# A new written order for the first two tiles of a windowed-attention and squared-ReLU kernel

## The chip, the cores and the metric

The kernel runs on one core of a Trainium2 chip. The metric is device time in microseconds (us) of one execution. The kernel before takes 847.6 us, the median of three executions (847.17 to 847.6).

## What is computed

The reference runs attention over a window of 64 positions and hands its output, seen as 4608 tokens of 512 values, to a feed-forward layer with a squared ReLU between two matrix products. All inputs are float32.

```python
scores = scale * np.matmul(q, k.transpose(0, 1, 3, 2))      # q, k, v: (8, 8, 576, 64)
mask = (rel >= 0) & (rel < window)                          # window = 64
attn = softmax(np.where(mask, scores, -1e9))
x = np.matmul(attn, v).transpose(0, 2, 1, 3).reshape(4608, 512)
h = x @ w_in                                                # (512, 2048)
r = np.maximum(h, 0.0)
out = (r * r) @ w_out                                       # (2048, 512)
```

## The kernel before

The 4608 tokens are cut into 12 tiles of 384. Attention is done in sections, three for each tile; a section is four pieces of 64 queries by two heads by two halves. The hidden size of 2048 is cut into 16 blocks f of 128. A wide product is made of three products of split operands: a high part and a rest.

Tiles 0 and 1 and the first two blocks of tile 2 are handled by a table of tokens, a string called `order` (line 488). It is walked once, from left to right, and every token issues its instructions at once to the queue of its engine; each engine then runs its own queue strictly in that order, and waits where data are missing. So the table fixes the order on TensorE, VectorE (DVE), ScalarE (ACT), GpSimd (POOL) and on SP, which issues all transfers. What follows the table is ordered by a planner with costs and due times (class Plan), which is not touched; its instructions follow the table's on every engine. Its first ones on TensorE are the first product of step 34, the scores of section 10 and the values of section 9.

A token is a letter, a number n and for some tokens the engine (d VectorE, a ScalarE, p GpSimd):

- Loads on SP: `L` and `N` q and k of 128 tokens of batch 0 and 1 (line 185), `w` the two halves of weight block n (lines 104, 105), `v` values (157), `q` raw q and k of later batches (147), `B` writes weight block n back to memory for later (519), `W` writes an output tile (457).
- Attention of the first tokens: `T`, `U` transposes on TensorE (196), `t`, `u` the copies out of their banks (202). `D` turns raw q and k of later batches on VectorE (167).
- Section n: `S` scores on TensorE (235), `o` copy of half of them (243), `s` the masked other half (252, 253), `z` row maximum (255), `y` its scaling, `e` and `f` four exponentials each on ScalarE (263), `k`, `R` the reciprocal of the sums (266, 269), `m` the weighting (272), `X` transposes (276), `x` their masked copy on VectorE (280), `V` product with the values (298), `H` the high part and `Q` the rest of the result (313, 315), which is the input of the feed-forward layer.
- Weight block n, which arrives as pairs of 32-bit words: `a` on ScalarE (118), `b` two instructions, `c`, `d` on VectorE (120, 121, 123, 125), `h` the high part on ScalarE (129), `l` the rest on VectorE (132). Two blocks at most are between `a` and `l`.
- Step n (a pair of tile and block): `M` the first product, 12 matmuls (404), into one bank that all steps share; `r` ReLU on ScalarE (413), `p` square (416 or 418), `g` high part on ScalarE (421), `G` rest on VectorE (423), `O` the second product, 9 matmuls (446). Steps 0 to 4 are tile 0 with blocks 0 to 4, steps 5 to 9 tile 1 with the same blocks, and steps 10 to 22 are tile 1 with blocks 5 to 15 and, in two of them, tile 0. Step 22 ends tile 1, step 31 tile 0; steps 32 and 33 are tile 2. `Z` copies the finished tile out (455).
- `K` n filler matmuls on constants, on TensorE (512), whose result nobody reads.

There are eight semaphores for the transfers in turn, so a transfer is issued only when the eighth one before it has landed.

Of the kernel before, what the change touches and what calls it, by code (L numbers as in the profile page):

```python
# [29 lines left out]
def window_attention_relu2_ffn(ctx: ExitStack, tc: tile.TileContext, q, k, v, w_in, w_out, out):  # L30
    nc = tc.nc
    pe, dve, act, pool, sp = nc.tensor, nc.vector, nc.scalar, nc.gpsimd, nc.sync
# [73 lines left out]


    def weight(op, f):
        if op == "a":
            wa[f] = a_t[:, f % 2].bitcast(I32)  # L110
        a = wa[f]
        if op in "acd":
            words = wraw[f].rearrange("p n (e w) -> p w (n e)", w=2)
            lower, upper = words[:, 0, :], words[:, 1, :]
        else:
            av = a.bitcast(F32).rearrange("p (n e) -> p n e", n=2)
        if op == "a":
            act.activation(a.bitcast(F32), upper.bitcast(F32), AF.Abs, scale=2.0 ** -80)
        elif op == "b":
            dve.tensor_scalar(a.bitcast(F32), a.bitcast(F32), 1.875 * 2.0 ** -64, 2.0 ** -95, ALU.min, ALU.max)  # L120
            dve.tensor_scalar(a, a, 4, 1, ALU.logical_shift_left, ALU.logical_shift_right)
        elif op == "c":
            dve.scalar_tensor_tensor(a, lower, 29, a, ALU.logical_shift_right, ALU.bitwise_or)  # L123
        elif op == "d":
            dve.scalar_tensor_tensor(a, upper, -0x80000000, a, ALU.bitwise_and, ALU.bitwise_or)  # L125
# [25 lines left out]
    def load_v(b, t, which=None):  # L151
        vt = vts[b, t] = vt_t[:, t]
        for n in range(min(2, NB - 2 * t)):
            s0 = (2 * t + n) * QB
            for m in range(2):
                if not which or (n, m) in which:
                    sp.dma_start(vt[m * QB:(m + 1) * QB, n],  # L157
                                 v[b, m * H // 2:(m + 1) * H // 2, s0:s0 + QB, :].rearrange("h s d -> s h d"))
# [251 lines left out]
    def evac(op, n, eng=None):  # L410
        if op == "r":
            rg[n] = r_t[:, n % 2]
            act.activation(by_half(rg[n]), ordered(hs.pop(n)), AF.Relu)  # L413
        elif op == "p":
            if eng == "a":
                act.activation(rg[n], rg[n], AF.Square)
            else:
                dve.tensor_tensor(rg[n], rg[n], rg[n], ALU.mult)
        elif op == "g":
            gs[n] = (ghi_t[:, n % 3], glo_t[:, n % 2])  # L420
            act.copy(gs[n][0], rg[n])  # L421
        else:
            dve.tensor_tensor(gs[n][1], rg.pop(n), gs[n][0].bitcast(F32), ALU.subtract)  # L423

# [63 lines left out]
    order = """
        L0 L1 w0 L2 T0 v0 T1 t0a t1d S0 w1 T2 o0a T3 K5 t2d v1 s0 t3d a0 z0 S1 L3 y0 b0 f0 N0 T4 K3 c0 o1a L4
        t4a s1 T5 K5 e0 w2 d0 t5a N1 k0 z1 h0 S2 R0 y1 v2 m0d e1 l0 X0 K6 o2a x0 a1 v3 s2 V0 f1 b1 H0a k1 T6 K4  # L490
        w3 z2 R1 y2 t6d m1p v4 f2 Q0 T7 X1 c1 t7a U0 e2 x1 S3 u0a k2 d1 V1 o3a T8 v5 H1a R2 s3 m2p t8a T9 a2 Q1
        X2 t9d z3 h1 U2 K2 w4 b2 y3 u2a U1 K4 f3 w5 x2 u1a w6 c2 U3 e3 S4 w7 l1 u3a V2 k3 o4a v6 R3 H2a s4 m3p
        Q2 S5 a3 z4 X3 o5a b3 M0 y4 f4 x3 e4 c3 V3 r0 k4 d2 p0a M1 v7 H3a g0 R4 Q3 m4p h2 s5 X4 r1 G0 p1a z5 O0
        g1 x4 y5 e5 G1 V4 d3 f5 O1 v8 l2 H4a k5 h3 R5 Q4 m5p M2 a4 l3 w8 w9 X5 r2 b4 a5 M3 w10 x5 p2a w11 g2 c4
        r3 V5 w12 p3a G2 g3 w13 d4 O2 w14 G3 h4 H5d O3 w15 l4 q0 Q5 a6 M4 b5 b6 r4 M5 p4a c5 g4 q1 c6 r5 M6 p5a
        G4 g5 d6 O4 r6 d5 h6 G5 p6a M7 h5 g6 l5 O5 r7 G6 a7 l6 p7a O6 b7 g7 a8 G7 M8 c7 b8 O7 r8 p8a d7 g8 M9 G8
        h7 c8 O8 r9 l7 p9a g9 d8 a9 M10 G9 h8 b9 O9 r10 l8 p10a g10 c9 a10 B0 M11 G10 b10 O10 r11 p11a d9 g11 B1
        M12 G11 h9 c10 O11 r12 l9 p12a g12 d10 a11 B2 M13 G12 h10 b11 O12 r13 l10 p13a g13 c11 a12 B3 M14 G13
        b12 O13 r14 p14a d11 g14 B4 M15 G14 h11 c12 O14 r15 l11 p15a g15 d12 a13 B5 M16 G15 h12 b13 O15 r16 l12
        p16a g16 c13 a14 B6 M17 G16 b14 O16 r17 p17a d13 g17 B7 M18 G17 h13 c14 O17 r18 l13 p18a g18 d14 a15 B8  # L500
        M19 G18 h14 b15 O18 r19 l14 p19a g19 c15 B9 M20 G19 D0 O19 r20 p20a d15 q2 g20 M21 G20 h15 D1 O20 r21
        l15 p21a g21 q3 G21 M22 O21 r22 p22d g22 G22 M23 D2 O22 r23 p23d q4 g23 M24 G23 Z22 W22 O23 r24 p24d g24
        G24 S6 M25 o6a D3 q5 s6 O24 r25 z6 p25a y6 g25 f6 G25 S7 O25 e6 o7d s7 v9 k6 z7 M26 R6 y7 m6p f7 D4 X6
        e7 q6 S8 x6 r26 k7 V6 R7 o8a p26d m7p M27 H6a s8 g26 Q6 z8 X7 r27 G26 y8 M28 p27a x7 e8 D5 O26 g27 f8
        G27 q7 V7 r28 k8 R8 p28a m8p S9 g28 H7d M29 G28 Q7 o9d v10 X8 r29 s9 M30 p29a x8 g29 z9 v11 V8 r30 D6 y9
        f9 M31 p30d H8a e9 Q8 O27 k9 R9 m9p G29 O28 g30 r31 p31d X9 G30 g31 O29 x9 D7 G31 M32 O30 r32 p32d g32
        M33 G32 O31 r33 Z31 W31 p33d g33 G33"""
# [588 lines left out]
```

## Time and profile before

| what | before |
|---|---|
| median of three executions | 847.6 us |
| the profiled execution | 847.38 us |
| its span, first to last instruction | 845.1 us |
| busy: TensorE, VectorE, ScalarE, GpSimd | 829.0, 590.5, 407.3, 184.9 us |
| first matmul of the table | 4.26 us |
| first product of step 0 (`M0`) starts | 39.85 us |
| last second product of the table (`O31`) starts, ends | 185.74, 187.68 us |
| mean granted TensorE clock | 0.998 |

The span is the time from the first to the last instruction; the 2.28 us between it and the execution's own time lie around it. Times in the timeline are from the start of the span. A matmul's end is modelled, so the distance from one start to the next tells more than a duration. A row's "idle before" is how long the engine had nothing to do, and the name behind the arrow is what ended it.

### The profile page before, as it was taken

The numbers are of one execution on the slowest core, as the hardware profiler recorded it, in microseconds if no ns is written. First come the engines' busy times: TensorE is split into PE (matmuls) and PEld (weight loads), VectorE is DVE, ScalarE is ACT, GpSimd is POOL, SyncE is SP. The second block draws the span as 40 slices with busy tenths as digits, with TensorE's granted clock in tenths as the row PEclk, the third lists the DMA queues.
The fourth block names the chain that finished last, engine by engine and source line by source line (L and its number), as shares of the span: only waits on it lengthen the run. The fifth ranks groups of instructions, "written<-read, shape, count | busy, mean of one in ns | idle before, by whom it ended". The sixth has DMA issues, their size and how long they took to land.

```text
span 845.1 us, 17706 instructions
## 1 busy us (share of the span) xinstructions
PE 829.0 (98%) x6754; PEld 761.2 (90%) x6754; DVE 590.5 (70%) x889; ACT 407.3 (48%) x1127; POOL 184.9 (22%) x239
## 2 busy tenths in 40 slices
PE   7899999999999999999999999999999999999998
PEld 5788989899999999999999999999999999999997
DVE  5899996746767866767687765788755668544553
ACT  5887874646446555544442354453454424222221
POOL 1220003204557420311320121141112132010110
PEclk9999999999999999999999999999999999999999
DMA  9989956584688875999896797999785556686411
GB/s 230 231 257 346 306 239 130 86 171 126 153 210 251 214 170 119 305 245 238 169 319 225 179 217 161 285 224 271 212 237 157 188 194 182 236 259 212 136 66 74
DMA packets 273012, 173.92 MB, mean 206 GB/s; under 512 B 190497, under 2 KB 239649, under 8 KB 270881
## 3 DMA queue, kind: packets, MB, share of 16 engines
q1 hardware_dynamic: 272928, 172.80, 73.8%
q8 instruction: 53, 0.87, 0.5%
q14 instruction: 31, 0.25, 0.1%
HBM read 138.15 MB, written 34.60 MB: 204 GB/s over the span
## 4 chain that ended last, share of the span: by engine, by line
PE 86%; SPq 5%; DVE 3%; DMA 3%; issue 2%; ACT 1%; POOL 0%; DVEq 0%; ACTq 0%; POOLq 0%
PE banks L993 29%; PE banks L912 26%; PE banks L446 11%; PE banks L404 11%; PE banks L235 3%; PE banks L298 3%; DMA w<-in_moe_w_out_dram 2%; PE banks L276 2%; SPq L147 1%; SPq L185 1%; SPq L157 1%; DVE a L123 1%; DVE a L125 1%; SPq L104 1%; DVE g L423 1%
## 5 line engine op out<-in xcount | busy, mean ns | idle before, releaser
L993 PE MATMUL banks<-w 128*128 128x512 f32 x1152 | 257.5, 380 | 0.0
L993 PEld LDWEIGHTS banks<-w 128*128 128x128 f32 x1152 | 215.7, 189 | 28.4
L404 PE MATMUL banks<-x,w 128*128 128x384 f32 x768 | 137.1, 328 | 1.9 <-ACT r L413 1.4
L446 PE MATMUL banks<-w,g 128*128 128x512 f32 x576 | 136.1, 382 | 0.2
L404 PEld LDWEIGHTS banks<-x,w 128*128 128x128 f32 x768 | 126.6, 189 | 6.1 <-ACT r L413 3.3
L912 PE MATMUL banks<-x,w 128*128 128x384 f32 x768 | 130.3, 326 | 0.0
L938 POOL TENSOR_TENSOR g<-g 128x384 f32<-128x384 f32 x64 | 59.5, 934 | 323.1 <-ACT g L949 308.2
L912 PEld LDWEIGHTS banks<-x,w 128*128 128x128 f32 x768 | 125.6, 189 | 0.0
L446 PEld LDWEIGHTS banks<-w,g 128*128 128x128 f32 x576 | 106.2, 189 | 14.4 <-DVE g L423 1.2
L263 ACT ACTIVATE sel<-sel,nm 128x64 f32<-128x64 f32 x272 | 90.8, 336 | 25.9 <-DVE nm L257 22.8
L912 PE MATMUL banks<-w 128*128 128x384 f32 x576 | 100.7, 329 | 0.0
L1001 DVE TENSOR_TENSOR w<-w,banks 128x512 f32<-128x512 f32 x72 | 49.5, 687 | 69.9 <-PE banks L993 69.9
L912 PEld LDWEIGHTS banks<-w 128*128 128x128 f32 x576 | 93.8, 189 | 1.9
L983 ACT CAST w<-w 128x512 fp32r<-128x512 f32 x48 | 29.8, 620 | 72.9 <-PE banks L993 72.9
L413 ACT ACTIVATE r<-banks 128x384 f32<-128x384 f32 x64 | 31.5, 492 | 66.8 <-PE banks L404 64.6
L983 ACT CAST w<-g 128x512 fp32r<-128x512 f32 x48 | 29.7, 621 | 62.2 <-PE banks L993 58.2
L272 POOL TENSOR_TENSOR sel<-sel,nm 128x512 f32<-128x512 f32 x33 | 36.1, 1095 | 107.3 <-ACT g L949 51.7
L263 ACT ACTIVATION_READ_ACCUMULATOR sel<-sel,nm 128x1 f32 x272 | 51.2, 188 | 0.0
L423 DVE TENSOR_TENSOR g<-r,g 128x384 fp32r<-128x384 f32 x64 | 37.6, 588 | 18.0 <-ACT g L421 9.7
L535 POOL TENSOR_TENSOR a<-w 128x256 f32<-128x256 f32 x28 | 24.9, 906 | 105.3 <-DVE w L132 79.6
L280 DVE TENSOR_TENSOR pt<-banks,masks 128x1024 f32<-128x1024 f32 x33 | 40.3, 1220 | 10.9 <-PE banks L276 10.9
L926 DVE TENSOR_TENSOR w<-banks,r 128x384 f32<-128x384 f32 x64 | 38.5, 601 | 13.3 <-PE banks L912 13.0
(103 smaller groups left out, 990.0 us busy)
## 6 DMA issues: line engine op xcount, KB each, us to landing
w<-mixed SPq DMA_DIRECT2D x128, 256.0 KB, 5.1
w<-kept SPq DMA_DIRECT2D x64, 512.0 KB, 7.2
w<-kept SPq DMA_DIRECT2D x96, 256.0 KB, 5.9
kept<-w SPq DMA_DIRECT2D x16, 1024.0 KB, 7.5
vt<-in_v_dram SPq DMA_DIRECT2D x144, 64.0 KB, 2.9
w<-in_moe_w_in_dram SPq DMA_DIRECT2D x16, 512.0 KB, 7.5
w<-in_moe_w_out_dram SPq DMA_DIRECT2D x16, 512.0 KB, 8.4
raw<-in_q_dram SPq DMA_DIRECT2D x112, 72.0 KB, 3.4
```

The source lines that it names most:

```text
L263: act.activation(sels[i][:, w, hd], sels[i][:, w, hd], AF.Exp, bias=nms[i][:, n], scale=SCALE, accum_out=sums[i][:, n])
L272: (dve if eng == "d" else pool).tensor_tensor(p, p, rs[i][:, :, None].broadcast_to([P, SW * 2, QB]), ALU.mult)
L280: dve.tensor_tensor(pts[i].rearrange("p (w n) q -> p w n q", n=2), ps_t[i][:, :, None, :].broadcast_to([P, SW, 2, P]), masks.rearrange("p ...
L404: pe.matmul(h_ps, lhsT=weights(kk, part), rhs=in_turn(x[xx][:, kk // 2, kk % 2]), start=n == 0, stop=n == 3 * NK - 1)
L423: dve.tensor_tensor(gs[n][1], rg.pop(n), gs[n][0].bitcast(F32), ALU.subtract)
L446: pe.matmul(acc(t, tb), lhsT=gg[:, ts], rhs=in_turn(weights(part)), start=f == 0 and n == 0, stop=f == NF - 1 and n == 2)
L912: pe.matmul(ps[:, :TT], lhsT=w[:, part, kk * P:(kk + 1) * P], rhs=in_turn(x[:, xx, kk]), start=n < 4 and m == 0, stop=m == 5, skip_group_c ...
L926: plan("dve", 0.6, lambda: dve.tensor_tensor(to(), ps, other(), ALU.add), [kps, ko], keys, 0, after)
L938: plan("pool", 0.95, lambda: pool.tensor_tensor(x(), x(), x(), ALU.mult), [], keys)
L983: plan("act", 0.62, lambda: act.copy(high(c), src()), g_keys, [kh], 0, freed("hi") if new else [])
L993: pe.matmul(ps, lhsT=gg[:, m // 2, m % 2], rhs=in_turn(wo_slot(w[m])[:, part]), start=m == 0 and n == 0, stop=m == 3 and n == 2)
L1001: plan("dve", 0.72, lambda: dve.tensor_tensor(by_half(parts(tb)), by_half(parts(tb)), ordered(ps), ALU.add), [key], [kp])
```

## The change

The table is replaced as a whole. The new one holds the same tokens except for these differences in the work: the copies `t2`, `t3`, `t6` and `t9` go from VectorE to ScalarE, the copy `H4` from ScalarE to VectorE, and the fillers go from 29 to 50, 25 of them in one piece (`K25`). The weight blocks, loaded from 0 to 15 in turn before, are now loaded in the order 0, 1, 2, 3, 4, 10, 8, 6, 5, 12, 14, 7, 9, 15, 11, 13. Three lines let more operations be sent to GpSimd; no token of the new table does so.

```diff
-    def weight(op, f):
+    def weight(op, f, eng=None):
...
-            dve.tensor_tensor(w[:, :, 1], av, w[:, :, 0].bitcast(F32), ALU.subtract)
+            (pool if eng == "p" else dve).tensor_tensor(w[:, :, 1], av, w[:, :, 0].bitcast(F32), ALU.subtract)
...
-                dve.tensor_tensor(rg[n], rg[n], rg[n], ALU.mult)
+                (pool if eng == "p" else dve).tensor_tensor(rg[n], rg[n], rg[n], ALU.mult)
...
-            dve.tensor_tensor(gs[n][1], rg.pop(n), gs[n][0].bitcast(F32), ALU.subtract)
+            (pool if eng == "p" else dve).tensor_tensor(gs[n][1], rg.pop(n), gs[n][0].bitcast(F32), ALU.subtract)
...
     order = """
-        L0 L1 w0 L2 T0 v0 T1 t0a t1d S0 w1 T2 o0a T3 K5 t2d v1 s0 t3d a0 z0 S1 L3 y0 b0 f0 N0 T4 K3 c0 o1a L4
...
-        M33 G32 O31 r33 Z31 W31 p33d g33 G33"""
+        L0 T1 t1d T0 t0a K2 S0 o0a s0 w0 a0 b0 z0 c0 w1 y0 L1 L2 K25 T3 a1 b1 f0 t3a d0 T2 t2a K2 S1 c1 w2 e0 k0
...
+        O31 Z31 G32 X9 W31 x9 D6 D7 v11 G33"""
...
-                weight(op, n)
+                weight(op, n, eng)
```

At the start, on SP and on TensorE. The first transfers before are `L0`, `L1`, `w0`, `L2`, `v0`, `w1`; in the piece of SP's difference, lines 104 and 105 are the two halves of a weight block, line 185 is q and k of a group of tokens.

```order
 L1091 UNCONDITIONAL_BRANCH
+L185 DMA w<-in_q_dram 128x8x64
+L185 DMA w<-in_k_dram 128x8x64
+L104 DMA w<-in_moe_w_in_dram 128x4x256
+L105 DMA w<-in_moe_w_out_dram 128x1024
+L104 DMA w<-in_moe_w_in_dram 128x4x256
+L105 DMA w<-in_moe_w_out_dram 128x1024
 L185 DMA w<-in_q_dram 128x8x64
 L185 DMA w<-in_k_dram 128x8x64
```

Weight blocks 0 and 1 now stand ahead of the second group of tokens. On TensorE line 196 is a transpose, line 235 scores, line 512 a filler.

```order
 L196 MATMUL banks<-ident,w 128x128 x8
+L512 MATMUL banks<-ident 128x128 x2
 L235 MATMUL banks<-qk 64x64 x4
 L235 MATMUL banks<-qk 64x128 x4
 L235 MATMUL banks<-qk 64x64 x4
 L235 MATMUL banks<-qk 64x128 x4
+L512 MATMUL banks<-ident 128x128 x25
 L196 MATMUL banks<-ident,w 128x128 x8
-L512 MATMUL banks<-ident 128x128 x5
-L235 MATMUL banks<-qk 64x128 x16
```

After the scores of section 0, the 25 fillers now stand ahead of the transposes `T3` and `T2`, on which the scores of section 1 depend.

At the end of the table, on TensorE and VectorE. First TensorE before, from `M33` over `O31` to the planner's step 34, section 10's scores (line 235) and section 9's values (line 298):

```order
L404 MATMUL banks<-x_1672,w 128x384 x12
L446 MATMUL banks<-w,g 128x512 x9
L404 MATMUL banks<-x_1672,w 128x384 x12
L235 MATMUL banks<-qk 64x64 x4
L235 MATMUL banks<-qk 64x128 x12
L298 MATMUL banks<-pt,vt 64x128 x12
```

The same place now:

```order
L404 MATMUL banks<-x_1736,w 128x384 x12
L446 MATMUL banks<-w,g 128x512 x9
L276 MATMUL banks<-ident,sel 128x128 x4
L404 MATMUL banks<-x_1736,w 128x384 x12
L235 MATMUL banks<-qk 64x64 x4
L235 MATMUL banks<-qk 64x128 x12
L298 MATMUL banks<-pt,vt 64x128 x12
```

The transposes of section 9 (`X9`, line 276), which stood three second products earlier, now come behind `O31`. VectorE before, from `x9` (line 280) to the table's last `G` (line 423):

```order
L280 TENSOR_TENSOR pt<-banks,masks 128x1024
L167 STREAM_TRANSPOSE qk<-raw 128x1152
L423 TENSOR_TENSOR g<-r,g 128x384
L418 TENSOR_TENSOR r<-r 128x384
L423 TENSOR_TENSOR g<-r,g 128x384
L418 TENSOR_TENSOR r<-r 128x384
L423 TENSOR_TENSOR g<-r,g 128x384
```

And now:

```order
L423 TENSOR_TENSOR g<-r,g 128x384
L418 TENSOR_TENSOR r<-r 128x384
L423 TENSOR_TENSOR g<-r,g 128x384
L280 TENSOR_TENSOR pt<-banks,masks 128x1024
L167 STREAM_TRANSPOSE qk<-raw 128x1152 x2
L423 TENSOR_TENSOR g<-r,g 128x384
```

`x9` and the turns `D6` and `D7` (line 167) now stand between the last but one and the last `G`. In the built program the scores of section 10 wait for `D6` and `D7`, and `x9` waits for `X9`.

At the end of the table, on SP. Before, the first row holds the values `v10` and `v11` (line 157), and raw q and k of later batches follow (line 147); the output of tile 0 (`W31`, line 457) comes 19 rows behind it:

```order
L157 DMA vt<-in_v_dram 64x4x64 x8
L147 DMA raw<-in_q_dram 32x18x32
L147 DMA raw<-in_k_dram 32x18x32
L147 DMA raw<-in_q_dram 32x18x32
L147 DMA raw<-in_k_dram 32x18x32
```

And now:

```order
L157 DMA vt<-in_v_dram 64x4x64 x8
L519 DMA kept<-w 128x2048
L457 DMA out_dram<-x_1969 128x512 x3
L157 DMA vt<-in_v_dram 64x4x64 x4
L147 DMA raw<-in_q_dram 32x18x32
L147 DMA raw<-in_k_dram 32x18x32
```

The first row is now `v10` and a load of the planner; `v11`, which section 9's values read, stands behind the output of tile 0, and that waits for the copies `Z31` of `O31`'s result.

More of the change, by code (lines that the diff above doesn't have):

```diff
@@ L488, in window_attention_relu2_ffn @@
     order = """
-        L0 L1 w0 L2 T0 v0 T1 t0a t1d S0 w1 T2 o0a T3 K5 t2d v1 s0 t3d a0 z0 S1 L3 y0 b0 f0 N0 T4 K3 c0 o1a L4
[L490 to L503, printed above, removed]
@@ L504, in window_attention_relu2_ffn @@
-        e7 q6 S8 x6 r26 k7 V6 R7 o8a p26d m7p M27 H6a s8 g26 Q6 z8 X7 r27 G26 y8 M28 p27a x7 e8 D5 O26 g27 f8
-        G27 q7 V7 r28 k8 R8 p28a m8p S9 g28 H7d M29 G28 Q7 o9d v10 X8 r29 s9 M30 p29a x8 g29 z9 v11 V8 r30 D6 y9
-        f9 M31 p30d H8a e9 Q8 O27 k9 R9 m9p G29 O28 g30 r31 p31d X9 G30 g31 O29 x9 D7 G31 M32 O30 r32 p32d g32
-        M33 G32 O31 r33 Z31 W31 p33d g33 G33"""
+        L0 T1 t1d T0 t0a K2 S0 o0a s0 w0 a0 b0 z0 c0 w1 y0 L1 L2 K25 T3 a1 b1 f0 t3a d0 T2 t2a K2 S1 c1 w2 e0 k0
@@ new lines, in window_attention_relu2_ffn @@
+        o1a s1 d1 z1 T4 t4a R0 h0 l0 m0d K2 T5 y1 t5a h1 K2 S2 l1 e1 K6 X0 x0 L3 T6 o2a s2 v0 v1 f1 k1 N0 w3 t6a
+        R1 a2 K4 V0 H0a T7 z2 b2 t7a L4 m1p X1 Q0 x1 y2 f2 v2 e2 c2 k2 R2 d2 S3 o3a s3 U0 u0a N1 V1 H1a w4 K2 T8
+        Q1 t8a T9 h2 t9a m2p z3 X2 x2 a3 b3 K2 U2 u2a v3 y3 f3 K3 U1 u1a V2 l2 H2a Q2 e3 c3 S4 U3 M0 w10 o4a a4
+        v5 s4 k3 R3 z4 b4 d3 y4 r0 p0a M1 g0 G0 u3a f4 w8 m3p X3 x3 c4 r1 S5 e4 k4 o5a p1a s5 v4 M2 R4 g1 G1 z5
+        h3 V3 H3a Q3 m4p l3 O0 X4 x4 y5 v6 e5 f5 O1 d4 k5 V4 H4d R5 Q4 r2 p2a h4 l4 w6 g2 m5p M3 G2 w5 X5 x5 r3
@@ new lines, in window_attention_relu2_ffn @@
+        M4 w12 a6 b6 p3a g3 r4 G3 V5 H5d Q5 O2 a5 b5 q1 c5 M5 c6 d5 w14 r5 p4a p5a g5 q0 O3 w7 g4 G4 h5 G5 M6 r6
+        p6a d6 h6 g6 l5 v9 l6 O4 a7 G6 b7 c7 v7 d7 M7 r7 O5 p7a g7 a8 M8 r8 B4 G7 w9 h7 O6 p8a g8 M9 r9 O7 p9a
+        g9 M10 b8 w15 l7 G8 O8 a9 c8 d8 h8 r10 G9 B1 B3 b9 p10a M11 B2 g10 O9 c9 l8 a10 r11 p11a g11 d9 w11 h9
+        w13 G10 b10 M12 r12 O10 c10 p12a g12 M13 l9 a11 G11 O11 d10 r13 M14 G12 O12 h10 p13a g13 r14 b11 c11 l10
+        a12 p14a G13 d11 D0 B5 b12 M15 h11 B9 l11 O13 r15 M16 p15a c12 g14 G14 O14 a13 r16 b13 p16a M17 g16 v8
@@ new lines, in window_attention_relu2_ffn @@
+        g15 d12 h12 G15 r17 c13 O15 p17a M18 g17 G16 l12 a14 O16 r18 p18a g18 d13 G17 b14 c14 h13 M19 d14 h14 q2
+        O17 l13 r19 M20 a15 G18 O18 r20 p20a l14 p19a b15 c15 d15 M21 g20 g19 G19 O19 h15 l15 r21 G20 M22 p21a
+        O20 D2 r22 M23 g21 G21 r23 O21 D1 q3 p23d g23 p22d G23 g22 G22 M24 r24 p24d g24 O22 B7 Z22 O23 q4 M25 S6
+        r25 p25a G24 o6a D3 g25 q5 s6 z6 y6 M26 r26 W22 p26d S7 D4 f6 e6 k6 M27 o7d g26 G25 r27 R6 s7 z7 y7 O24
+        G26 M28 S8 m6p X6 p27a g27 f7 D5 x6 r28 o8a s8 z8 O25 e7 M29 G27 S9 r29 p29a y8 e8 V6 H6a Q6 O26 M30 B6
@@ L508, in window_attention_relu2_ffn @@
+        k7 R7 B0 f8 m7p X7 x7 g29 O27 k8 R8 m8p V7 p28a g28 G28 r30 p30d O28 g30 H7d Q7 X8 B8 G29 M31 r31 x8 V8
+        o9d s9 z9 H8a Q8 y9 f9 p31d g31 O29 G30 q7 q6 M32 r32 O30 p32d M33 v10 e9 k9 R9 g32 G31 r33 m9p p33d g33
+        O31 Z31 G32 X9 W31 x9 D6 D7 v11 G33"""
     ps_f = {}
```

## The prediction

> **Bound now.** I read the page first: span, then the busy tenths.
>
> ```profile
> span 845.1 us, 17706 instructions
> ...
> PE   7899999999999999999999999999999999999998
> ...
> DVE  5899996746767866767687765788755668544553
> ...
> GB/s 230 231 257 346 306 239 130 86 171 126 153 210 251 214 170 119 305 245 238 169 319 225 179 217 161 285 224 271 212 237 157 188 194 182 236 259 212 136 66 74
> ```
>
> A slice is 21.1 us. TensorE (PE) is full from the third slice on; VectorE (DVE) is full only in slices three to six, and the table ends in slice nine. So what the table decides is when TensorE begins, whether VectorE holds it up, and how cleanly it hands over to the planner's part, which is the same in both and full: a shift at the handover should reach the end. 2.28 us lie outside the span (847.38 less 845.1); the profiled execution is 0.2 us under the median, so a sum against it stands for the median too.
>
> Next the windows over the table (busy us of PE, PEld, DVE, ACT and POOL, then granted clock, DMA share, GB/s).
>
> ```profile
> 40.00:73.00 33.00, 31.07 (x295) 27.64 (x295) 31.53 (x38) 25.76 (x65) 4.60 (x6) 1.00 0.92 295
> 73.00:130.00 57.00, 56.79 (x303) 52.34 (x302) 56.47 (x63) 44.31 (x60) 0.00 (x0) 1.00 0.78 272
> ```
>
> From 40 to 73 VectorE is idle for 1.5 us and TensorE for 1.9; from 73 to 130 neither has more than 0.6. They bind together, so VectorE's work ahead of a product is the thing to count.
>
> TensorE's timeline at the end of the table and just behind it, starts in the first column:
>
> ```profile
> 177.51 0.60 PE L276 MATMUL banks<-ident,sel 128*128 128x128 f32 x4
> 177.87 2.19 PE L446 MATMUL banks<-w,g 128*128 128x512 f32 x9
> ...
> 183.78 2.11 PE L404 MATMUL banks<-x,w 128*128 128x384 f32 x12
> ...
> 185.74 2.11 PE L446 MATMUL banks<-w,g 128*128 128x512 f32 x9
> ...
> 187.68 2.11 PE L404 MATMUL banks<-x,w 128*128 128x384 f32 x12
> ...
> 189.72 1.00 PE L235 MATMUL banks<-qk 64*64 64x64 f32 x32
> ...
> 190.54 0.95 PE L298 MATMUL banks<-pt,vt 64*64 64x128 f32 x32
> ...
> 191.42 2.21 PE L446 MATMUL banks<-w,g 128*128 128x512 f32 x9
> ```
>
> `O31` (185.74) runs straight into the planner's product, section 10's scores, section 9's values and the next product. From start to start a first product takes 1.96 us, a second 1.94, a section's transposes 0.36, its scores 0.82, its values 0.88. No wait stands here: any wait that the new order puts here is new.
>
> **The start.** The new order puts weight blocks 0 and 1 ahead of the second group of tokens, works on them on VectorE at once, and lets TensorE run `K25` ahead of `T3` and `T2`.
>
> ```profile
> 10.47 1.75 PE L512 MATMUL banks<-ident 128*128 128x128 f32 x10
> 12.16 1.10 PE L235 MATMUL banks<-qk 64*64 64x128 f32 x32
> ...
> 18.95 1.50 PE L512 MATMUL banks<-ident 128*128 128x128 f32 x12
> ...
> 27.09 1.08 PE L298 MATMUL banks<-w,vt 64*64 64x128 f32 x48
> ...
> 39.85 2.20 PE L404 MATMUL banks<-x,w 128*128 128x384 f32 x12
> ```
>
> A token's filler leaves two records. At 10.47 ten take 1.69 us, 0.17 each; at 18.95 twelve take 1.50, 0.125 each. The 50 of `K25` therefore take between 6.25 and 8.5 us; with the first few at 0.17 and the rest at 0.125 I take 7.1. Section 0's scores end at about 9.6 in the new order (before they start at 7.01, with one group of fillers less ahead), so `K25` ends at 16.7, `T3` and `T2` at 17.9, their copy at 18.5, section 0's last exponentials, behind that copy on ScalarE, at 19.8, section 1's copy `o1a` at 20.3. Only then can VectorE mask section 1 (`s1`); it has been idle for 2.3 us by then, because its weight work on blocks 0 and 1 is out of material (`c1` ends at about 18).
>
> The Trainium skill, "TensorE: Matmul & The Clock Gate", section "What's actually happening", says that the array runs at half rate until about 3.4 us of sustained work have passed. Sustained work began here with the transposes at about 5.3, so by that rule all of `K25` would run at 0.125 and the sum would be some 0.9 us lower; the 0.17 at 10.47, five us after, speak against it, and the measurement decides.
>
> From `s1` on VectorE is the chain. Its rows:
>
> ```profile
> 25.60 1.21 DVE L280 TENSOR_TENSOR w<-banks,masks 128x1024 f32<-128x1024 f32 x1
> 26.73 1.21 DVE L125 SCALAR_TENSOR_TENSOR a<-w,a 128x1024 int32<-128x1024 int32 x1
> ...
> 73.05 0.55 DVE L423 TENSOR_TENSOR g<-r,g 128x384 fp32r<-128x384 f32 x1
> ...
> 126.33 1.37 DVE L167 STREAM_TRANSPOSE qk<-raw 128x1152 f32<-128x1152 f32 x1
> 127.62 1.44 DVE L125 SCALAR_TENSOR_TENSOR a<-w,a 128x1024 int32<-128x1024 int32 x1
> ...
> 191.67 0.58 DVE L253 COPY_PREDICATED sel<-late,banks 128x384 f32<-128x384 int32 x1
> 192.29 0.69 DVE L255 TENSOR_REDUCE nm<-sel 128x8 f32<-128x512 f32 x1
> ```
>
> A 1024-wide operation takes 1.13 us from start to start, a turn of raw q and k 1.29, a half-width one 0.62. From `s1` to `Q2`, which `M0` needs, the new order has nine long ones (`d1 l0 l1 x0 x1 c2 d2 x2 l2`: 10.2), fourteen half-width ones (`s`, `z` and `Q` three each, `m0d`, `b2` and `b3` two each: 8.7) and three reciprocals (0.4): 19.3. From 20.3 that gives 39.6 to 40.0: `M0` starts where it started before, 39.85. Cost of the start: 0 (bounds -0.9 with all fillers at 0.125, +1.4 with all at 0.17).
>
> **From `M0` to `O31`.** What is different is how far VectorE is by then. From `Q2` to `G6` with `l6`, the old order still has 17 long operations and `b3`; the new has 15, because `d2` and `l2` lie ahead of `Q2`, but `s4` and `H4d` in addition. That is 2 times 1.13 plus 2 times 0.62 less 2 times 0.62: VectorE is 2.3 us ahead by then, and `G6`, done at 73.6 before (the row at 73.05), is done at 71.3. TensorE must be able to take it up. Its ledger, by spacing: from 39.85 to 187.68 are 147.8 us, and 34 first products, 32 second, four scores, six values (up to 1.0 by the 48-record row at 27.09) and six transposes make 34 x 1.96 + 32 x 1.94 + 4 x 0.82 + 6 x 1.0 + 6 x 0.36 = 140.2. So 7.6 are lost to waits, more than the idle columns show, because modelled ends hide part. Where they lie:
>
> ```profile
> 61.35 2.11 PE L404 MATMUL banks<-x,w 128*128 128x384 f32 x12
> ...
> 64.04 2.22 PE L404 MATMUL banks<-x,w 128*128 128x384 f32 x12 [0.58 <-ACT r L413]
> ...
> 66.84 2.22 PE L404 MATMUL banks<-x,w 128*128 128x384 f32 x12 [0.58 <-ACT r L413]
> ```
>
> Adjacent first products share one bank, so the second waits for the ReLU of the first: 2.69 instead of 1.96, 0.73 lost each time. The old order has such runs (`M4 M5 M6`) because `G` was not ready; the new one spreads the products from `M5` on as M, O, M, O, and has runs only at `M0 M1` and `M3 M4`, with attention between. It adds section 5's scores and section 3's transposes to this stretch and takes section 9's transposes out: +0.8. I take 2.9 us of the 7.6 as recovered: 2.1 us gained, `O31` ending at 185.6. It is just under VectorE's lead of 2.3, its ceiling, and the lower bound is 0.7 (only the 1.9 idle of 40 to 73, less 1.2 of work added there). If nothing is recovered this term is +0.8.
>
> **The handover.** Behind `O31` TensorE now has section 9's transposes `X9`, then the planner's product, then section 10's scores, which wait for the turns `D6` and `D7`, then section 9's values, which wait for `v11`. Counted from the end of `O31` as zero: `X9` ends at 0.6. `x9` on VectorE runs from there, the next starts at 1.76 (1.13 later), `D7` at 3.05 (1.29), and ends at 4.4 (1.37). The scores could start at 0.36 + 1.95 = 2.3 and start at 4.45: 2.1 us lost.
>
> For the values I need ScalarE and SP.
>
> ```profile
> 186.46 0.56 DVE L418 TENSOR_TENSOR r<-r 128x384 f32<-128x384 f32 x1 [1.84 <-ACT r L413]
> 186.58 1.88 ACT L455 COPY x<-banks 128x512 f32<-128x512 f32 x3 [0.16 <-PE banks L446]
> 187.20 1.62 SPq L457 DMA_DIRECT2D out_dram<-x  x3
> ...
> 188.36 0.52 ACT L421 CAST g<-r 128x384 fp32r<-128x384 f32 x1
> ...
> L157 SPq DMA_DIRECT2D vt<-in_v_dram x144: 595/611/3260, 6.9 to 629.0; - x144
> DMA to landing us min/median/max: 2.3/2.9/11.2
> ```
>
> `g33` now stands ahead of the copies `Z31`, so these end at about 1.8 rather than 0.8, and the third output transfer leaves SP at 1.9. The four loads of `v11` follow at 0.61 each; the last is issued at about 3.7 and lands 2.3 to 2.9 later, at 6.0 to 6.6. The values would follow the scores at 5.3 and end at 6.2; now at least their last part waits until then, and they end at 6.2 to 7.2, against 4.0 without a wait. The handover costs 2.1 to 3.1, I take 2.6. Behind this wait on TensorE stand the second products of the planner, behind `v11` on SP raw q and k for later sections, which have tens of us. The copies `t2`, `t3`, `t6`, `t9` and `H4` that changed engine are inside the counts above.
>
> **Sum**: 0 - 2.1 + 2.6 = +0.5, 847.38 + 0.5 = 847.9 us.
>
> **Rivals.** (1) *Weight block 7 comes late; slower.* It is now the twelfth block to load, behind blocks 10, 8, 12 and 14. Ahead of it and with it go 12 blocks of 1.05 MB, 4.85 MB of tokens and values and 1.18 MB of raw q and k: 18.6 MB. At the first three slices' mean of 239 GB/s that takes until 78, at the window's 295 GB/s until 63; late in the stretch only large blocks are left, so I expect 70. ScalarE wants it (`a7`) about when `G6` is done, at 71.3; `r7` is queued behind `a7`, and `M8` behind `r7` by the shared bank. From then on each us late costs TensorE one; landing at 75.3 it is 847.9 + 4 = 852.0. For it: the tokens and values, in rows of 256 bytes, come first, and the DMA share is 0.92 already. Against: the old order was fed up to 73 at 295.
>
> (2) *The clock falls before `M0`; slower.* The new order has few fillers between section 2 and `M0`.
>
> ```profile
> 32.00:33.00 1.00, 0.68 (x4) 0.39 (x3) 0.96 (x3) 1.00 (x5) 0.00 (x0) 0.50 0.36 82
> ```
>
> The old order lost the clock at 32 to 33, granted 0.50, in a thin stretch. If the values of section 2 and the scores of section 4 run at half rate, that is 1.0 + 0.8 on the way to `M0`: 847.9 + 1.8 = 849.7. Against it: VectorE, not TensorE, sets `Q2`, and may cover it. The Trainium skill, the same page, section "HAM oscillation — how this bites in real kernels", names idle gaps of over about 3.4 us as what takes the clock away; by that nothing would fall here, and this row, with no gap of that size near it, disagrees.
>
> (3) *The start is ahead; faster.* If `K25` runs at 0.125 throughout, `M0` comes 0.9 earlier, and if TensorE then keeps 1.6 fewer of the 4.7 us of losses left, `O31` ends 4.6 earlier: 847.38 - 4.6 + 2.6 = 845.4. For it: the rate of 0.125 from 18.95. Against: the rate of 0.17 at 10.47.
>
> (4) *The handover's waits are absorbed; faster.* If the planner's part has waits on TensorE that a later start only fills (16.1 us of the span are idle), only the gain stays: 847.38 - 2.1 = 845.3. Against: no idle stands in the rows from 187.68 to 191.42, and nothing later is due to the handover.
>
> **Numbers.** Of this kernel a measurement tells 0.2%, 1.7 us, from no change. Forecast 0.38 (no change, 847.9; its own range 845.9 to 849.3), block 7 late 0.20, clock 0.15, start ahead 0.17, absorbed 0.10. Faster 0.27, same 0.38, slower 0.35. For 8 in 10 I take 844.0 to 852.0: it holds the forecast with its bounds (0 to -2.3 and 2.1 to 3.1) and all rivals at their price, and leaves out a late block beyond 76 and both gains together.
>
> **What would show it.** `M0` at 39.5 to 40.2 and VectorE idle before `s1` near 18 to 20: the start is right. `G6` done at about 71.3 and `O31` ending at about 185.6: the lead. Section 10's scores waiting 2 us on line 167, and section 9's values on a load of line 157: the handover. An idle ScalarE ahead of line 118 near 71, released by a weight load, with TensorE idle behind it, is rival 1; a clock of 0.50 between 33 and 41 is rival 2; `M0` before 39 is rival 3; the handover's waits present but the rest of the span shorter by as much is rival 4. A `M0` later than 41 or a gain over 3 us by `O31` would make the forecast wrong at its root.

## The result

The changed kernel takes 858.09 us, the median of four executions (856.49 to 859.22), against 847.6: a ratio of 1.0119, 95% interval 1.0096 to 1.0142. It is 10.5 us slower. The forecast was no change (847.9), and the time lies above the range (844.0 to 852.0). The profiled execution took 858.88 us with a span of 856.9, 11.8 more than before, and where they are can be read off TensorE's timeline, because from the planner's first second product on both take the same to the end (653.7 us).

| stretch of TensorE | before | changed | difference | predicted |
|---|---|---|---|---|
| start to `M0` | 39.85 | 44.59 | +4.7 | 0 |
| `M0` to the end of `O31` | 147.8 | 151.7 | +3.9 | -2.1 |
| end of `O31` to the next second product | 3.7 | 6.9 | +3.1 | +2.6, and 0.4 for `X9` |

Only the handover is as predicted.

### The profile page after: what moved, and what is told of

Read it like the earlier page. It is cut to its first block, busy times and chain, and to the rows that moved or that the text cites. A ratio compares the mean times of both kernels' runs of the same rounds, so it can differ in the third digit from the quotient of the medians.

```text
span 856.9 us, 17766 instructions
## 1 busy us (share of the span) xinstructions
PE 836.4 (98%) x6796; PEld 768.5 (90%) x6796; DVE 590.1 (69%) x886; ACT 404.8 (47%) x1130; POOL 187.3 (22%) x239
## 4 chain that ended last, share of the span: by engine, by line
PE 85%; SPq 6%; DVE 3%; DMA 2%; ACT 2%; issue 1%; ACTq 0%
PE banks L993 29%; PE banks L912 26%; PE banks L446 11%; PE banks L404 11%; PE banks L235 3%; PE banks L298 3%; SPq L147 2%; PE banks L276 2%; SPq L185 1%; SPq L157 1%; DVE a L123 1%; DVE a L125 1%; DMA w<-in_moe_w_out_dram 1%; DMA kept<-w 1%; DMA w<-in_k_dram 1%
## 5 line engine op out<-in xcount | busy, mean ns | idle before, releaser
L931 DVE SCALAR_TENSOR_TENSOR w<-w 128x384 f32<-128x384 f32 x64 | 46.3, 724 | 1.7
```

Of the source, the lines that this page charges most:

```text
L931: plan("dve", 0.57, lambda: dve.scalar_tensor_tensor(x(), x(), 0.0, x(), ALU.max, ALU.mult), [], keys)
```

## The profile after

From the page of the changed kernel, the span, the busy tenths of TensorE, the rate of the transfers, and the group of the first products with the idle time ahead of them:

```profile
span 856.9 us, 17766 instructions
...
PE   7798999999999999999999999999999999999998
...
GB/s 244 215 275 235 358 98 25 281 143 130 197 180 247 185 230 95 286 265 188 205 289 239 211 232 163 287 204 230 254 226 136 225 185 153 265 244 212 133 75 75
...
L404 PE MATMUL banks<-x,w 128*128 128x384 f32 x768 | 138.8, 331 | 4.0 <-ACT r L413 3.9
```

The page hardly shows it: one tenth less for TensorE in the second and in the fourth slice (a slice is 21.4 us here), and 4.0 us of idle time ahead of first products where the old order had 1.9. The timeline of TensorE in the changed kernel shows the three places:

```profile
29.98 0.33 PE L196 MATMUL banks<-ident,w 128*128 128x128 f32 x1 [0.61 <-DMA w<-in_q_dram]
...
35.02 0.25 PE L196 MATMUL banks<-ident,w 64*128 64x64 f32 x1 [1.90 <-DMA w<-in_q_dram]
...
44.59 2.51 PE L404 MATMUL banks<-x,w 128*128 128x384 f32 x12
...
78.17 2.11 PE L446 MATMUL banks<-w,g 128*128 128x512 f32 x9
83.16 3.49 PE L404 MATMUL banks<-x,w 128*128 128x384 f32 x12 [2.88 <-ACT r L413]
86.44 2.56 PE L446 MATMUL banks<-w,g 128*128 128x512 f32 x9
88.83 2.11 PE L404 MATMUL banks<-x,w 128*128 128x384 f32 x12
...
196.33 0.60 PE L276 MATMUL banks<-ident,sel 128*128 128x128 f32 x4
196.69 2.20 PE L404 MATMUL banks<-x,w 128*128 128x384 f32 x12
199.53 0.33 PE L235 MATMUL banks<-qk 64*64 64x64 f32 x4 [0.65 <-DVE qk L167]
200.79 0.98 PE L235 MATMUL banks<-qk 64*64 64x64 f32 x27 [0.93 <-DVE qk L167]
...
202.91 0.33 PE L298 MATMUL banks<-pt,vt 64*64 64x64 f32 x4 [0.37 <-DMA vt<-in_v_dram]
```

First, the transposes of the last token groups wait for their loads (`U0` for `N0`, then `T8` for `L4`). Second, `M8` waits from 80.1 to 83.2 and then takes 3.28 us to the next start instead of 1.96. Third, the handover waits for the turns and for `v11`, as the prediction had it. The first two go back to SP. Its issues before:

```profile
13.40 3.38 SPq L157 DMA_DIRECT2D vt<-in_v_dram  x4
...
18.26 0.91 SPq L185 DMA_DIRECT2D w<-in_q_dram  x1
...
20.42 1.06 SPq L185 DMA_DIRECT2D w<-in_q_dram  x1
```

And in the changed kernel:

```profile
17.01 8.47 SPq L157 DMA_DIRECT2D vt<-in_v_dram  x8
25.52 0.61 SPq L185 DMA_DIRECT2D w<-in_q_dram  x1
...
29.19 0.60 SPq L185 DMA_DIRECT2D w<-in_q_dram  x1
...
55.25 0.72 SPq L147 DMA_DIRECT2D raw<-in_q_dram  x1
...
74.73 0.44 SPq L104 DMA_DIRECT2D w<-in_moe_w_in_dram  x1
```

`N0` leaves SP at 25.5 rather than 18.3 and `L4` at 29.2 rather than 20.4, behind the eight loads of `v0` and `v1`, which hold SP for 8.5 us. Block 7 (74.7) stands behind 16 loads of raw q and k and block 14, which begin at 55.3. ScalarE and VectorE then wait for it:

```profile
81.60 1.12 ACT L118 ACTIVATE a<-w 128x1024 f32<-128x1024 f32 x1 [3.86 <-DMA w<-in_moe_w_out_dram]
```

```profile
82.75 0.69 DVE L120 TENSOR_SCALAR a<-a 128x1024 f32<-128x1024 f32 x1 [3.71 <-ACT a L118]
```

## The experiments

The theory after the first look: all of the loss but the handover is the order of loads on SP, a load standing in front of a more urgent one. The rival: the memory itself is short, so that moving a load only makes another late. Each ratio below is to the kernel before on the same chip; for the changed kernel it is 1.0119. The chips differ by up to 1.3 us in the kernel before (847.6 to 848.9), so a difference of two medians from two chips is uncertain by about as much; the places in the timeline, from one profile each, tell more.

**One part undone at a time.** Only the loads of the last token groups earlier:

```diff
-... X0 x0 L3 T6 o2a s2 v0 v1 f1 k1 N0 w3 t6a ... t7a L4 m1p ... y2 f2 v2 e2 ... u0a N1 V1 ...
+... X0 x0 L3 N0 L4 T6 o2a s2 v0 v1 N1 f1 k1 w3 v2 t6a ... t7a m1p ... y2 f2 e2 ... u0a V1 ...
```

> The changed kernel with only the loads of the last token groups (L4, N0, N1) put ahead of the values v0 to v2 on SP. Theory: M0 is late (44.6 instead of 39.9) because the transposes of those groups wait for loads that SP issues late, so M0 comes at about 40. But the load of block 7 keeps its place behind 16 loads of raw q and k, so ScalarE then waits longer for it and M8 comes hardly earlier: 854 to 858. Rival (the memory, not SP's order, is short): M0 stays at 43 to 45, since the values are late instead. Rival (the two losses simply add): M0 at 40 and the whole time 4.7 less, 853.4.

857.63 us, ratio 1.0104 (1.0089 to 1.0119).

```profile
40.88 2.50 PE L404 MATMUL banks<-x,w 128*128 128x384 f32 x12
...
81.79 3.90 PE L404 MATMUL banks<-x,w 128*128 128x384 f32 x12 [5.18 <-ACT r L413]
```

`M0` came 3.7 us earlier and `M8` only 1.4: the gain ran into block 7, whose time is set by SP's queue (it left SP at 74.7 in both). As the theory said; that the losses simply add, which would have given 853.4, is refuted.

Only block 7 ahead of block 12:

```diff
-... G2 w5 X5 x5 ... g5 q0 O3 w7 g4 ...
+... G2 w5 w7 X5 x5 ... g5 q0 O3 g4 ...
```

> The changed kernel with only the two halves of weight block 7 put ahead of block 12 and of the raw q and k on SP. Theory: its place in SP's queue alone is what made it late; it lands near 62, ScalarE does not wait, M8 does not wait and does not run at half clock (3.0 of wait and 1.8 of clock): 858.1 - 4.8 = 853.3. Rival (memory too slow): it lands later than 77 still, or another block is late in its place, 856 to 858.

857.84 us, ratio 1.0103 (1.0088 to 1.0118): the rival's time. The 2.9 us ahead of `M8` are gone, but ScalarE now waits 2.0 us for a later block at 89.3 (block 9 left SP at 81.5), and TensorE 0.5 to 0.8 at five places from 92 to 131. From `M0` to the end of `O31` it is 150.8 instead of 151.7. So block 7 alone was not the cause. The new theory: the loads of raw q and k delay every block behind them.

Both blocks that come late, 7 and 9, earlier, and those loads (with the values `v9` and `v7`) later:

```diff
-... G2 w5 X5 x5 r3 M4 w12 a6 ... a5 b5 q1 c5 ... g5 q0 O3 w7 ... l5 v9 l6 ... c7 v7 d7 ... B4 G7 w9 ... d9 w11 h9 ...
+... G2 w5 w7 X5 x5 r3 M4 w12 w9 a6 ... a5 b5 c5 ... g5 O3 ... l5 l6 ... c7 d7 ... B4 G7 ... d9 w11 q1 q0 v9 v7 h9 ...
```

> The changed kernel with weight blocks 7 and 9 ahead on SP and the 16 loads of raw q and k and the values v9 and v7 put behind block 11. Theory: those loads, which hold SP for some 25 us between 55 and 81, are what makes every block behind them late (in the run with block 7 moved alone, block 9 came late in its place); with them out of the way no block is late, no first product waits over 1 us from 70 to 130, and the time is 858.1 - 4.8 = 853.3. Rival (the memory is full, whatever SP's order): another block comes late, ScalarE waits over 3 us for blocks between 60 and 110, 856 to 858.

855.03 us, ratio 1.0078 (1.0057 to 1.0098), 3.1 us less than the changed kernel, where the theory had 4.8; one wait of 0.7 and one of 0.4 are left between 70 and 130.

```profile
44.48 2.51 PE L404 MATMUL banks<-x,w 128*128 128x384 f32 x12
...
192.56 0.60 PE L276 MATMUL banks<-ident,sel 128*128 128x128 f32 x4
```

From `M0` to the end of `O31` it is now 148.1 (192.56 less 44.48): the late blocks cost 3.7, not the 4.8 that the wait and the products at half clock had suggested. And with no late block the stretch is no shorter than the 147.8 of the old order. The predicted gain of 2.1 is not there.

**The clock.** Why 3.7 and not 4.8? Ten fillers on a bank that is idle there, between `O5` and `M8`:

```diff
-... O5 p7a g7 a8 M8 ...
+... O5 p7a g7 a8 K110 M8 ...
...
-        for _ in range(n):
-            pe.matmul(banks[:, 4, :P], ...)
+        for _ in range(n % 100):
+            pe.matmul(banks[:, 3 if n > 99 else 4, :P], ...)
```

> The changed kernel with 10 fillers on an idle bank between O5 and M8, 2.5 us of work in the 3 us in which TensorE waits for block 7. Theory (the clock falls because TensorE idles for 3 us): the granted clock stays at 1.00 from 83 to 88, M8 takes 1.96 from start to start rather than 3.28 and O6 1.95 rather than 2.39, the time is 1.8 less, about 856.3. Rival (the clock falls for another reason, or the fillers push M8 back): M8 over 3 us again or starting later by as much, 857.5 to 859.

858.16 us, ratio 1.0111 (1.0089 to 1.0132). The window from 84 to 86 (PE, PEld, DVE, ACT, POOL busy, granted clock, DMA share, GB/s) in the changed kernel, then with the fillers, then TensorE's timeline with the fillers:

```profile
84.00:86.00 2.00, 2.00 (x8) 2.00 (x7) 1.93 (x3) 1.26 (x2) 0.00 (x0) 0.50 1.00 333
```

```profile
84.00:86.00 2.00, 2.00 (x13) 1.92 (x12) 1.93 (x3) 2.00 (x3) 0.00 (x0) 1.00 0.94 304
```

```profile
80.20 2.39 PE L512 MATMUL banks<-ident 128*128 128x128 f32 x20
83.17 2.22 PE L404 MATMUL banks<-x,w 128*128 128x384 f32 x12 [0.58 <-ACT r L413]
85.23 2.11 PE L446 MATMUL banks<-w,g 128*128 128x512 f32 x9
87.17 2.11 PE L404 MATMUL banks<-x,w 128*128 128x384 f32 x12
...
100.30 2.22 PE L404 MATMUL banks<-x,w 128*128 128x384 f32 x12 [0.75 <-ACT r L413]
```

On the mechanism the theory was right: the clock stays at 1.00, `M8` takes 2.06, and `M9` starts 1.7 earlier. On its worth it was wrong: the end of `O31` is at 196.26 against 196.33, and the time is the same. (`M0` came 0.7 later in this run, but by `O5` the two were level, 78.26 and 78.17.) VectorE had lost 3.7 us to the same late block, and TensorE waits for it further on: the ReLU behind the wait at 100.3 follows work on ScalarE that had waited 1.9 us for VectorE. The lower clock lay inside VectorE's delay and cost at most 0.2.

**The handover.** `D6` and `D7` into VectorE's idle time, `v11` ahead of the output:

```diff
-... O30 p32d M33 ... G31 r33 m9p p33d g33 O31 Z31 G32 X9 W31 x9 D6 D7 v11 G33
+... O30 p32d D6 M33 ... G31 D7 r33 m9p p33d g33 v11 O31 Z31 G32 X9 W31 x9 G33
```

> The changed kernel with only the turns D6 and D7 put into VectorE's idle time ahead of O31 and the values v11 ahead of the output of tile 0. Theory: the waits of section 10's scores and section 9's values are worth 2.7 us, which reach the end: 855.4. Rival (the planner's part absorbs them): 857.5 to 858.5.

855.35 us, ratio 1.0077 (1.0062 to 1.0092): 2.7 less, as expected. From the end of `O31` to the next second product it is 4.2 (194.62 to 198.80) instead of 6.9, which is the 2.7. That the medians differ by just as much is in part luck: the profile's span is 3.6 shorter, with 1.7 gained ahead of the end of `O31` and 0.8 lost again behind the handover (the last wait, below).

The other way round, the old kernel with only the new end:

```diff
-... g29 z9 v11 V8 r30 D6 y9 ... p31d X9 G30 g31 O29 x9 D7 G31 ... O31 r33 Z31 W31 p33d g33 G33
+... g29 z9 V8 r30 y9 ... p31d G30 g31 O29 G31 ... O31 r33 p33d g33 Z31 X9 W31 x9 D6 D7 v11 G33
```

> The kernel before with only the end of the table as in the changed one: X9, x9, D6 and D7 behind O31, v11 behind the output of tile 0, g33 ahead of Z31. Theory: the scores of section 10 and the values of section 9 wait as there, next second product 6.8 us after O31 rather than 3.7, less what the products gain by X9 moving (0.4): 2.6 to 3.1 more, 850.3 to 851. Rival (the planner's part absorbs it): 847.5 to 848.5.

852.03 us, above the expected 850.3 to 851, ratio 1.0052 (1.0028 to 1.0076): slower by 2.4 to 6.4 us by the interval, in which 2.6 to 3.1 lie. The profile shows the rest: `M0` came at 41.16, 1.3 later than in the profile of the kernel before, although the start is the same.

```profile
191.70 0.33 PE L235 MATMUL banks<-qk 64*64 64x64 f32 x4 [0.65 <-DVE qk L167]
192.96 0.98 PE L235 MATMUL banks<-qk 64*64 64x64 f32 x27 [0.93 <-DVE qk L167]
...
195.18 0.33 PE L298 MATMUL banks<-pt,vt 64*64 64x64 f32 x4 [0.46 <-DMA vt<-in_v_dram]
195.44 2.21 PE L446 MATMUL banks<-w,g 128*128 128x512 f32 x9
```

The same waits as in the changed kernel; `O31` ends at 188.5 there, so it is 6.9 to the next second product. From there to the end of the span it takes 653.7, as in the kernel before. So the handover's price is shown from both sides, and the planner's part absorbs none of it.

**All three, and the first loads.** The three edits together:

> All three edits together. Theory: 858.1 - 4.7 - 4.8 - 2.7 = 845.9, just under the kernel before, because VectorE's lead of about 1 us is then left. Rival (memory short, the losses move elsewhere): 850 or more.

856.33 us (853.23 to 857.85), ratio 1.0076 (1.0052 to 1.0100): the rival's time, and no better than the handover alone. In the profile, which is of the slowest of the four executions, `M0` was at 44.9 again, although the loads stood as in the run that had it at 40.9. This time `V0` waited 2.1 us for `v0` and ScalarE 3.3 us for block 3. The first loads had indeed traded places, so the question was the order of all of them. `v0` ahead, block 2 behind the token groups:

```diff
-... L1 L2 K25 ... S1 c1 w2 e0 ... x0 L3 T6 o2a s2 v0 v1 f1 k1 N0 w3 t6a ... L4 m1p ... v2 e2 ... N1 V1 ...
+... L1 L2 v0 K25 ... S1 c1 e0 ... x0 L3 N0 L4 w2 T6 o2a s2 v1 N1 f1 k1 w3 v2 t6a ... m1p ... e2 ... V1 ...
```

> The changed kernel with the first loads only in another order: v0 ahead of L3, the token groups L4 and N0 ahead of weight block 2. Theory: with the large block 2 behind them the last token groups and v0 land in time, M0 at 40 to 41; block 7 keeps its place, so M8 then waits 5 us or more, as in the run with L4, N0, N1 moved, and the whole time is 856 to 858. Rival: now block 2 or 3 is late and ScalarE, which runs in order, holds the attention up: M0 at 43 or later.

857.61 us, ratio 1.0103 (1.0082 to 1.0124), `M0` at 42.6: between the two. With the blocks and the handover added:

> These two edits together, with D6 and D7 in VectorE's idle time and v11 ahead of the output of tile 0. Theory (the start costs 4, late blocks 4.8, the handover 2.7, all by SP's order but for the turns): 858.1 - 11.5 = 846.6, one us under the kernel before. Rival (loads only trade places): over 850.

851.08 us (849.4 to 855.04), ratio 1.0037 (1.0019 to 1.0054), the rival's time; `M0` at 41.8, and ScalarE waited 2.3 us for block 2 ahead of it. With block 2 between `L3` and `N0`:

```diff
-... x0 L3 N0 L4 w2 T6 ...
+... x0 L3 w2 N0 L4 T6 ...
```

> As the run with all parts (first loads reordered, blocks 7 and 9 early, raw q and k late, handover undone), but weight block 2 stands ahead of N0 and L4 and behind v0 and L3. There ScalarE waited 2.3 us for block 2 and M0 came at 41.8. Theory (the first loads only trade places: any order that puts 2 MB of weights ahead makes one of them late): M0 at 40.5 to 43 again, the time 850 to 852. Rival (it is a matter of the right order): M0 at 39.5 to 40.2, the time 849.

849.97 us (848.03 to 852.09), ratio 1.0020 (1.0006 to 1.0035), `M0` at 40.4. It falls between the theory (loads only trade places) and the rival (a matter of the right order), just at the edge of the theory in `M0` and in time. So the order of the first loads is worth 4 us of `M0` (44.6 to 40.4), but no order tried brought it to 39.85. The window from 20 to 28, in the old kernel, in the changed one, and in this run:

```profile
20.00:28.00 8.00, 6.79 (x141) 5.50 (x139) 7.91 (x11) 7.29 (x30) 2.54 (x4) 1.00 1.16 254
```

```profile
20.00:28.00 8.00, 7.05 (x105) 6.00 (x104) 7.35 (x11) 7.15 (x24) 2.87 (x4) 1.00 0.58 132
```

```profile
20.00:28.00 8.00, 7.05 (x105) 6.01 (x104) 7.34 (x11) 7.16 (x23) 2.66 (x4) 1.00 1.19 264
```

The changed order moves 132 GB/s there, while SP works through eight small loads in a row, and the repaired one 264. But the lull only moved: from 12 to 20 the two move 241 and 163 GB/s, and over 12 to 36 they move 210 and 217. What the repair changed is which loads come first, and hardly how much is moved. Both rates are far below the 358 GB/s of the changed kernel's own fifth slice, so no run shows the memory as the limit here; none shows either that these small loads could go faster.

One more try at the same cause, `v0` and `v1` issued by ScalarE early on, behind `a0` and `a1` (with the blocks and the handover repaired):

```diff
-                    sp.dma_start(vt[m * QB:(m + 1) * QB, n],
+                    (act if b == 0 and t < 2 and not which else sp).dma_start(vt[m * QB:(m + 1) * QB, n],
```

> The changed kernel with blocks 7 and 9 early, raw q and k late, the handover undone, and the first values v0 and v1 issued by ScalarE early on rather than by SP; SP's other loads keep their order. Theory (what delays N0 and L4 is SP's eight issues for v0 and v1, 8.5 us from 17.0 to 25.5): N0 leaves SP 6 to 8 us earlier, M0 at 40 to 41. Rival (the memory is what is short before 40 us): N0 and L4 land no earlier than 28 and 33, M0 at 43 or later.

859.77 us, ratio 1.0122 (1.0093 to 1.0150). `N0` did leave SP 7.6 us earlier (at 18.0), but as a test of the start this one failed, with `M0` at 50.4: the issues on ScalarE wait for earlier transfers as they do on SP, ScalarE stood still behind them, and section 1's scores waited 10.2 us for its copy.

```profile
27.64 1.99 PE L235 MATMUL banks<-qk 64*64 64x128 f32 x32 [10.23 <-ACT qk L202]
```

**The fillers.** By the prediction `K25` set the start. Cut to 5:

```diff
-... L1 L2 K25 T3 ...
+... L1 L2 K5 T3 ...
```

> The changed kernel with the 25 fillers after section 0's scores cut to 5. By the prediction's chain (fillers, then T3 and T2, then section 0's last exponentials, then section 1) section 1's mask on VectorE, 18.9 in the changed kernel, would come up to 4 us earlier. By the trace of the changed kernel ScalarE's exponentials f0, which wait for the row maximum until 14.7, come ahead of the copies of T3 and T2, so the fillers cost nothing: the mask stays at 18.5 to 19.2 and M0 at 44 to 45, the time 857 to 859.

857.3 us, ratio 1.0098 (1.0069 to 1.0127), `M0` at 43.9 and the mask of section 1 at 19.8, not earlier. These fillers cost nothing that shows; TensorE waited in their place (1.3 us for a load at 12.6).

**The last wait.** In the runs with the handover repaired, ScalarE's next use of the output's buffer waited for the output's transfer, and TensorE behind it. In the run before:

```profile
195.04 0.58 ACT L313 CAST x<-banks 128x512 fp32r<-128x512 f32 x1 [2.03 <-DMA out_dram<-x]
```

```profile
199.71 2.22 PE L404 MATMUL banks<-x,w 128*128 128x384 f32 x12 [0.95 <-ACT r L413]
```

The output moved ahead of four loads on SP, and `D6`, `D7`, `p33` and `g33` behind `O31`:

```diff
-... D6 M33 ... G31 D7 r33 m9p p33d g33 v11 O31 Z31 G32 X9 W31 x9 G33
+... M33 ... G31 r33 m9p O31 Z31 v11 W31 D6 D7 p33d g33 G32 X9 x9 G33
```

> As the best run so far (first loads, blocks 7 and 9, raw q and k, handover), but at the handover Z31 and its output stand ahead of D6 and D7, so the output of tile 0 leaves SP four loads of raw q and k earlier. In that run ScalarE's next use of the tile's buffer waited 2.0 us for the output's transfer near 195, and a first product near 200 waited for the ReLU behind it, 1.1 us. Theory (the repair of the handover made that wait by where it put the output on SP): ScalarE's wait is under 0.5, no wait of TensorE over 0.5 near 200, and the time is 1.1 less: 848.9, no different from the kernel before. Rival (the wait comes from something else behind the handover): TensorE waits at 200 as there, 850.

850.42 us (848.39 to 852.19), ratio 1.0031 (1.0018 to 1.0044).

```profile
194.24 0.59 ACT L313 CAST x<-banks 128x512 fp32r<-128x512 f32 x1 [0.80 <-DMA out_dram<-x]
```

```profile
199.02 2.11 PE L404 MATMUL banks<-x,w 128*128 128x384 f32 x12
```

In the trace the theory holds in the main: ScalarE waits 0.8 (under 0.5 was expected) and TensorE not at all, and the span is 846.8 against 847.5, with `M0` 0.3 later. In the timed runs the 1.1 us cannot be told from the spread; the expected 848.9 was not reached. Neither of the two repaired versions beats the kernel before.

## Why the prediction was wrong, point by point

**The start, 0.** Measured +4.7, with `M0` beyond the 41 that the prediction had named as the mark of being wrong at its root. The chain that it followed, fillers, `T3` and `T2`, section 0's exponentials, section 1's mask on VectorE, ended 1.4 us too late: the mask ran at 18.94, not at 20.3. The fillers took 5.7, not 7.1 and less than the 6.25 that was allowed at the least (0.114 a record), and did not gate it in any case: ScalarE was in exponentials that waited for the row maximum until 14.7.

```profile
14.71 0.35 ACT L263 ACTIVATE sel<-sel,nm 128x64 f32<-128x64 f32 x1 [1.20 <-POOL nm L257]
```

The step that failed comes next: "From `s1` on VectorE is the chain". The sum took VectorE's operations from `s1` to `Q2` as one run without a gap. They were counted right: 19.3 us in the sum, 19.8 measured. But from the mask to the end of `Q2` (44.98) are 26.0 us, and 6.3 of them are waits. The longest is ahead of `x2`, which needs the transposes `X2`; they stand on TensorE behind `T8`, which waited for `L4`:

```profile
38.24 1.22 DVE L280 TENSOR_TENSOR pt<-banks,masks 128x1024 f32<-128x1024 f32 x1 [3.25 <-PE banks L276]
```

The next is ahead of `Q2` itself, at 44.29 (its row is below): 2.4 us, for section 2's values on TensorE. SP's queue was checked for block 7 and for `v11`, but not for the last token groups, which had moved from 18 to 26 and from 20 to 29. The late loads are the largest term of the start, shown by the runs that move loads alone.

Rival 2, the clock, came as well, by its own sign (0.50 between 37 and 42). The window from 36 to 44 in the changed kernel and in the run with `M0` at 40.9:

```profile
36.00:44.00 8.00, 7.54 (x103) 6.74 (x106) 3.65 (x4) 5.24 (x15) 0.00 (x0) 0.57 1.14 273
```

```profile
36.00:44.00 8.00, 6.50 (x111) 5.40 (x110) 6.88 (x11) 6.98 (x23) 0.79 (x2) 1.00 1.01 291
```

From `X2` to `M0` TensorE ran without a wait in the changed kernel, and took 7.5 us (37.09 to 44.59), 2.4 of them the fillers `K2` and `K3`. In the run with `M0` at 40.9 the same work took 5.9 (34.95 to 40.88), of which 0.9 was a wait. By these two spacings I estimate the clock's part at 1.6 us or more, near the 1.8 of the rival. Against it the prediction had set that VectorE "may cover it"; it did not, because here TensorE's own queue was the chain. The few fillers that the rival named are not enough to bring the clock down: the three runs with `M0` between 40.4 and 40.9 have the same ones there, and a clock of 1.00 in this window. It fell where TensorE had waited for the late loads. No run has these late loads without the fall, so how the 4.7 divides stays an estimate.

**`M0` to `O31`, -2.1.** Measured +3.9, of which 3.7 are the late blocks (rival 1) by the run that takes them away. The rival had mechanism and place right, and was given 0.20. That it also had the size, a block 4 us late where ScalarE waited 3.9, is in part luck: it priced a landing at 75.3 against a need at 71.3, and the block was there by 81.6 against a need at 77.7, late itself by the start. With `M0` at 40.9 the wait ahead of `M8` was 5.2. What the rival missed is what set the landing: not 18.6 MB over one rate, but the 16 raw loads that hold SP in front of the block, at 0.4 to 2.7 us an issue.

The other 0.2 are what is left of the forecast -2.1 without a late block: if the 0.8 of added work holds, some 0.5 of the 2.9 us that the prediction counted as recovered waits were recovered. The step "VectorE is 2.3 us ahead by then" failed. VectorE in the old kernel, `Q2` and `l6`:

```profile
38.33 0.69 DVE L315 TENSOR_TENSOR x<-banks,x 128x512 fp32r<-128x512 f32 x1
...
73.52 1.22 DVE L132 TENSOR_TENSOR w<-a,w 128x1024 fp32r<-128x1024 f32 x1
```

And in the changed one, `Q2`, `d3` and `G6`:

```profile
44.29 0.69 DVE L315 TENSOR_TENSOR x<-banks,x 128x512 fp32r<-128x512 f32 x1 [2.36 <-ACT x L313]
...
48.99 2.06 DVE L125 SCALAR_TENSOR_TENSOR a<-w,a 128x1024 int32<-128x1024 int32 x1
...
78.50 0.55 DVE L423 TENSOR_TENSOR g<-r,g 128x384 fp32r<-128x384 f32 x1
```

`G6` and `l6` are both done 34.5 after `M0` in the new order and 34.9 in the old: a lead of 0.4. The operations between `Q2` and `G6` were counted right; the reference point was not. In the old order `M0` starts 1.5 after `Q2`, in the new 0.3, and those 1.2 us of VectorE's work had been credited to the new order. For the remaining 0.7 there is only an argument: single operations ran longer, as the 2.06 at 48.99, but the old order has one of 1.80 too. That TensorE's extra scores and transposes, +0.8, then took what lead there was is counted, not tested; with no late block the stretch is 148.0 to 148.2 in five runs, against 147.8.

**The handover, +2.6.** Right in every step. The scores start at 3.2 after the end of `O31` and again at 4.46 (predicted 4.45, with four of them going ahead after `D6`), the values' last part at 6.6 (6.0 to 6.6), and the whole costs 6.85 less 3.74 less the 0.36 of `X9`: 2.75.

**Rivals 3 and 4** did not happen: the start was behind, although the condition of rival 3, fast fillers, came true, and the handover's price reached the end both ways round.

The cases were treated as exclusive, each added to the forecast alone. Rivals 1 and 2 came together, with late token loads that no rival listed, and the range had no room for a sum.

## What to carry to other kernels

When an order is changed, walk SP's queue from front to back and write down for each load when it left before, when it can leave now, and when it is wanted; a load that is wanted early should not stand behind a row of small ones. When a lead is counted in operations between two marks, check that the marks stand equally far from the point that you shift by. And read a slow stretch on one engine against the delay of the others: the products at half clock behind `M8` cost nothing, because VectorE was late by more from the same cause, while the half clock ahead of `M0` cost, by the estimate above, some 1.6 us or more, because there TensorE's own queue was the chain.
